# A fused attention and two-MoE kernel: the column transfers of the first chunk put ahead of the transfers of x

## The chip, the cores and the metric

The kernel runs on one core of one Trainium2 chip. The metric is the device time of an execution in microseconds (us). The core has five engines that each run their own instructions in program order: TensorE (PE; its weight loads are listed apart as PEld), VectorE (DVE), ScalarE (ACT), GpSimd (POOL) and SyncE (SP). Nearly all data transfers (DMAs) are issued by SP, in SP's order. Each of SP's transfers signals one of eight completion counters, taken in turn and named DMAHW0 to DMAHW7 in the order rows below; a transfer that takes a counter waits until the transfer that had it before has landed.

## The reference

Attention with 4 batches, 8 heads, 576 positions and 64 channels, where heads 0 to 3 see the last 32 positions and heads 4 to 7 every 32nd one; then a dense MoE layer with a squared ReLU; then a routed layer of 8 experts of which each token takes one:

```python
def _moe2_ref(x, w_gate, w_output_gate, w1, w2):
    logits = x @ w_gate
    e_idx = np.argmax(logits, axis=1)
    ...
    eom = 1.0 / (1.0 + np.exp(-(x @ w_output_gate)))
    out = np.zeros((N, D), dtype=np.float32)
    for e in range(E):
        mask = e_idx == e
        ...
        h = np.maximum(x[mask] @ w1[e], 0.0)
        ye = h @ w2[e]
        out[mask] = gate_w[mask, None] * eom[mask, e, None] * ye
    return out

x = attention(q, k, v) as (2304, 512)
h = x @ w_in
r = np.maximum(h, 0.0)
x = (s * (r * r) + b) @ w_out
out = _moe2_ref(x, ...)
```

## The kernel before

The 2304 tokens are cut into five units of 256, 512, 512, 512 and 512 (`USZ`). Attention and the dense layer run unit by unit; each unit's result x goes to DRAM as `xd[u]` (line 1528). Matmuls are in float32 split in two parts, three products for each.

The routed layer bets on one expert. After the third unit the kernel takes the expert that most tokens chose and runs *all* tokens through that expert's weights (`dense`, from line 1924). For units 1 to 4 the first of its two matrix products is done in seven products of half size (M1 to M7, `product`, line 1975), which DVE and ACT combine (`combine`, line 1858). Such a stage on TensorE is: M1 and M6 of a stage, two products with the second matrix for the stage before (line 1940), M7 and M5, one more of those, M2, M4 and M3, and one more. On DVE a stage is `su` (line 1883), `dd` (lines 1886, 1889 and 1894) and the `ht` of line 1847. M7 waits for `su` of line 1883, and the next stage's M1 for the buffer that `dd` of line 1894 frees. Four stages make a unit; those of unit 2, the third one, lie around the change.

The operands of a unit come from `load_x` (line 1777): two transfers `xr` from `xd[s]` (line 1804), four sums `tt` on DVE (line 1818), and splits of them (lines 1661 and 1665) that the seven products read.

Tokens of other experts are then done in chunks of 32 (`SLOT`). `index` (line 2089) builds on DVE and TensorE a table of 80 columns, one for each chunk: `gid` has the token numbers, `sid` the places to write to, both in DRAM (lines 2192 and 2193). `li` holds the expert of each chunk and the number of chunks; its first column goes to DRAM as `lsd` (line 2204) and comes back as the row `lrow` (line 2205), from which the loop at the end takes a chunk's expert. `extra` (line 2209) does a chunk: it loads all of x into `X1` with five transfers (line 2213), reads the chunk's expert, loads the chunk's column as `gr` (line 2219), four times as `gc` (line 2221) and once from `sid` (line 2222), makes addresses `gs` on DVE (lines 2227 to 2229) for a gather by POOL, copies the 32 tokens out of `X1` into `xe` in eight groups of four (line 2242), each after a read of four numbers of `gr`, loads the expert's weights `we` in eight transfers (line 2249) into the buffer that `X1` had, and multiplies (lines 2260 to 2290). The first chunk is part of the schedule (`first_extra`, line 2302); any others follow in a loop (line 2358), which on this input has no turn.

The order of the work is not written out. `body` runs its parts as generators: each `yield op(...)` names an engine, a duration and the events waited for, and `Order` (line 211) keeps a clock for each engine and lets the part go on whose next step can start first, corrected by a priority. The order so found, with durations that are the source's own, is the order in which each engine gets its instructions. An event is an `Ev` whose time is set by `o.set`.

Of the kernel before, what the change touches and what calls it, by code (L numbers as in the profile page):

```python
# [6 lines left out]
F32 = mybir.dt.float32  # L7
F32R = mybir.dt.float32r
I32 = mybir.dt.int32
# [5 lines left out]
DVE = mybir.EngineType.DVE  # L15
# [3 lines left out]
NT, DM, DFF, E, DFE = B * S, H * D, 2048, 8, 1024  # L19
NF2 = DFE // 128  # L20
QT = 128
USZ = (256, 512, 512, 512, 512)
UOF = tuple(sum(USZ[:k]) for k in range(len(USZ) + 1))
# [12 lines left out]
P = 128  # L36
# [5 lines left out]
KD = DM // P  # L42
NF = DFF // P
NU = len(USZ)
# [29 lines left out]
P_ATT2 = 0.1  # L74
P_GATE = -0.2
P_EXTRA = 0.3
P_EXTRA_PE = -0.3
GLAT = 0.5
P_SUMS = 0.2
# [117 lines left out]
DMA_LAT = 1.8  # L197
# [114 lines left out]
def op(*engs, waits=(), dep=True, on=(), late=0.0):  # L312
    return engs, waits, dep, on, late
# [6 lines left out]
def body(ctx, tc, qkv, w12, moe_s, moe_b, wg, e12, out):  # L320
    nc = tc.nc
# [6 lines left out]
    const = enter(tc.tile_pool(name="const", bufs=1))  # L328
    wp = enter(tc.tile_pool(name="w", bufs=2 * NF))
    mx = enter(tc.tile_pool(name="mx", bufs=2))  # L330
# [6 lines left out]
    xd = [dram.tile([P, KD, USZ[u]], F32, name=f"xd{u}") for u in range(NU)]  # L337
# [3 lines left out]
    lsd = dram.tile([P, 1], I32, name="lsd")  # L341
# [49 lines left out]
    o = Order()  # L391
# [71 lines left out]
    t_g, t_r, t_raw, t_x1, t_c = Tok(NG), Tok(NR), Tok(NRAW), Tok(1), Tok(1)  # L463
# [546 lines left out]
    ev_last = [Ev() for _ in range(NU)]  # L1010
# [644 lines left out]
    def parts(src, dst, late=0.0):  # L1655
        n = 1
        for x in src.shape[1:]:
            n *= x
        yield op(("ACT", n / 1200 + 0.2), ("DVE", n / 1400 + 0.06, P_DVE), late=late)
        if o.eng == "ACT":  # L1660
            nc.scalar.activation(out=dst[0], in_=src, func=AF.Copy)
        else:
            nc.vector.tensor_copy(out=dst[0], in_=src)
        yield op(("DVE", n / 960 + 0.15))
        nc.vector.tensor_sub(out=dst[1], in0=src, in1=dst[0].bitcast(F32))
# [103 lines left out]
    def x_tile(shape):  # L1769
        tok = [t for t in o.got if t in (t_xa, t_xb, *t_xc.values())][0]  # L1770
        for b in t_xc:
            if tok is t_xc[b]:
                return st[b], tok
        pool, n = (m2[0], NXA) if tok is t_xa else (m2b[0], NXB)
        return pool.tile(shape, F32R, name="x2", tag="x2", bufs=n), tok

    def load_x(s):
        n = USZ[s]
        hn = n // 2
        yield op(("SP", 0.0), waits=[ev_k[4 * NF + 8], ev_last[s]])  # L1780
        raws = []
        if s == 0:
            yield op(("DMA", 2 * n / 350), waits=[t_w])
            t = wp.tile([P, KD, n], F32, name="xr", tag="w")
            nc.sync.dma_start(out=t, in_=xd[s])
            ev = Ev()
            o.set(ev, o.fin + DMA_LAT + 1.0)
            for c, b in enumerate(t_xc):
                def go(c=c, b=b):
                    yield op(("SP", 0.0), waits=[ev, ev_kept], dep=False)  # L1790
                    x = st[b]
                    yield from parts(t[:, 2 * c:2 * c + 2, :], [x[:, h] for h in range(2)])
                    x2[s, c] = x
                    if len(x2) == 2:
                        o.free(t_w)
                        o.set(ev_x2[s, "X"])
                        o.spawn(load_x(1), prio=P_X2)

                o.spawn(go(), prio=P_X2)
            return  # L1800
        for c in range(2):
            yield op(("DMA", n / 350), waits=[t_w])
            t = wp.tile([P, 2, n], F32, name="xr", tag="w")
            nc.sync.dma_start(out=t, in_=xd[s][:, 2 * c:2 * c + 2, :])
            ev = Ev()
            o.set(ev, o.fin + DMA_LAT + 1.0)
            raws.append((t, ev))
        (r0, e0), (r1, e1) = raws
        src = {"B11": r0[:, :, 0:hn], "B21": r1[:, :, 0:hn], "B22": r1[:, :, hn:]}
        w = 2 * hn / 960 + 0.15  # L1810
        yield op(("DVE", w), waits=[e0, e1, t_g, t_g])
        tt = [mx.tile([P, 2, 2, hn], F32, name="tt", tag="g", bufs=NG) for _ in range(2)]
        for k, b in enumerate(("T1", "T2", "T3", "T4")):
            src[b] = tt[k // 2][:, k % 2]
        for k, (x, y) in enumerate(((r0[:, :, hn:], src["B11"]), (src["B22"], src["T1"]), (src["B22"], r0[:, :, hn:]), (src["B21"], src["T2"]))):
            if k:
                yield op(("DVE", w))
            nc.vector.tensor_sub(out=tt[k // 2][:, k % 2], in0=x, in1=y)
        for b in OPS:
            yield op(("SP", 0.0), waits=[[t_xa, t_xb, *t_xc.values()]])  # L1820
            x, x_tok[s, b] = x_tile([P, 2, 2, hn])
            x2[s, b] = x

            def go(b=b, x=x):
                yield op(("SP", 0.0))
                yield from parts(src[b], [x[:, h] for h in range(2)])
                o.set(ev_x2[s, b])
                src.pop(b)
                if not src:
                    for _ in range(2):  # L1830
                        o.free(t_w)
                        o.free(t_g)
                    if s + 1 < NS:
                        o.spawn(load_x(s + 1), prio=P_X2)

            o.spawn(go(), prio=P_X2)
# [247 lines left out]


    ex = {}
    ev_idx = Ev()

    def index():
        yield op(("POOL", 2.5))  # L2090
# [71 lines left out]
        for t in range(0, NQT + 2, 2):  # L2162
            if t < NQT:
                yield op(("DVE", 0.5), waits=[t_w])
                ow = wp.tile([P, 1024], F32R, name="ow", tag="w")
                for k in range(2):
                    a = ow[0:QT, k * 512:k * 512 + SLOT]
                    c = ow[0:QT, k * 512 + SLOT:k * 512 + SLOT + NTAB]
# [22 lines left out]
        yield op(("DMA", 1.0))  # L2191
        nc.sync.dma_start(out=gid, in_=gi)
        nc.sync.dma_start(out=sid, in_=si2)
        yield op(("DVE", 0.7))
        before = tb[0:QT, 888:888 + E - 1]
        nc.vector.tensor_scalar(out=before, in0=end[:, 0:E - 1], scalar1=jc, scalar2=None, op0=ALU.is_le)
# [2 lines left out]
        li = const.tile([P, 2], I32, name="li")  # L2199
        nc.vector.tensor_copy(out=li[:, 0:1], in_=ej)  # L2200
        nc.vector.tensor_copy(out=li[:, 1:2], in_=end[:, E - 1:])
        yield op(("DMA", 3.0))
        lrow = const.tile([1, P], I32, name="lrow")
        nc.sync.dma_start(out=lsd, in_=li[:, 0:1])
        nc.sync.dma_start(out=lrow, in_=lsd.rearrange("(o s) c -> o (s c)", o=1))
        ex["li"], ex["lrow"] = li, lrow
        o.spawn(first_extra(), prio=P_EXTRA, pe=P_EXTRA_PE)

    def extra(col, get, n=NT):
        src = mx.tile([P, KD, NT], F32, name="X1", tag="big", bufs=1)  # L2210
        for u in range(NU):
            yield op(("DMA", 1.7), waits=[ev_last[u]])
            nc.sync.dma_start(out=src[:, :, UOF[u]:UOF[u + 1]], in_=xd[u])
        yield op(("DMA", 3.0))
        e = get()
        gr = mx.tile([1, SLOT], I32, name="gr", tag="gr", bufs=1)
        gc = mx.tile([P, 2], I32, name="gc", tag="gc", bufs=1)
        with nc.allow_non_contiguous_dma(reason="one column of a table"):
            nc.sync.dma_start(out=gr, in_=col(gid).rearrange("s o -> o s"))
            for h in range(NROW):  # L2220
# [10 lines left out]
        se = mx.tile([P, 1], F32, name="se", tag="se", bufs=1)  # L2231
        nc.gpsimd.indirect_dma_start(out=se, out_offset=None, in_=scd,
                                     in_offset=bass.IndirectOffsetOnAxis(ap=gs[:, 2:3], axis=0))
        yield op(("DVE", 1.8), waits=[t_r])
        xe = mx.tile([P, KD, SLOT], F32, name="xe", tag="r", bufs=NR)
        for k in range(0, SLOT, 4):
            if k:
# [5 lines left out]
        big = mx.tile([P, NF2, 1024], F32, name="we", tag="big", bufs=1)  # L2243
        we = []
        evs = []
        for fc in range(NF2):
            yield op(("DMA", 1.46))
            t = big[:, fc, :]
            nc.sync.dma_start(out=t, in_=e12[bass.ds(e * NF2 + fc, 1)].rearrange("o p f -> p (o f)"))
            we.append(t)  # L2250
            evs.append(Ev())
            o.set(evs[-1], o.fin + DMA_LAT)
        hp = None
        for k in range(NF2 // NROW):
            yield op(("PE", 1.0), waits=[evs[NROW * k + NROW - 1]] + ([t_att] if k == 0 else []))
# [39 lines left out]
        if n < NT:  # L2295
# [3 lines left out]
                                     in_=oe, in_offset=None, bounds_check=n - 1, oob_is_err=False)  # L2299
        o.free(t_g)  # L2300

    def first_extra():
        li = ex["li"]
        yield from extra(lambda t: t[:, 0:1], lambda: sp_value(li[0:1, 0:1], E - 1), NT - P)
# [31 lines left out]
    with tc.manual_schedule():  # L2336
        prep()
        o.filler = filler
        o.pe_cold = PE_COLD
        o.spawn(load_qkv(0), after=False)  # L2340
        o.spawn(load_w64(0), after=False)
        o.spawn(attn(0), prio=P_ATT, after=False)
        o.spawn(masks(1), after=False)
        o.spawn(split_w64(0), prio=P_SPLIT, after=False)
        o.spawn(moe1(), after=False)
        o.spawn(split_x0(), after=False, prio=P_X0)
        o.spawn(open_st(), after=False)
        o.spawn(make_ops(STR[0]), prio=P_OPS, after=False)
        o.spawn(open_m2(), after=False)
        o.spawn(make_sums(0), after=False, prio=P_SUMS)  # L2350
        if WARM:
            o.spawn(warm(), after=False, prio=P_WARM)
        o.spawn(load_x(0), prio=0.1, after=False)
        o.run()
    n = nc.values_load(ex["li"][0:1, 1:2], min_val=0, max_val=NTAB, skip_runtime_bounds_check_because=why)
    o.got = [t_att[0]]
    att_bank()
    with tc.For_i(1, n, 1) as j:
        lrow = ex["lrow"]
# [90 lines left out]
```

## Time and profile before

| | |
|---|---|
| median of 3 runs | 676.94 us (676.92 to 678.75) |
| profiled execution | 675.04 us |
| its span, from the first to the last instruction | 673.3 us |
| PE busy | 660.1 us (98%) |
| PEld busy | 570.7 us (85%) |
| DVE busy | 423.8 us (63%) |
| ACT busy | 317.7 us (47%) |
| granted TensorE clock | 1.000 |
| DMA | 83.81 MB, mean 124 GB/s |

Busy time is a mean over the span; a stretch in which an engine waits has to be looked for in the views by time. Times in those views count from the span's start. In a row of the timeline the first two numbers are start and duration of a group of equal instructions, xN their number, and the brackets at the end give how long the engine sat idle before it and what ended that. SPq rows are the issues of transfers: their duration is that of the issue, not of the transfer.

### The profile page before, as it was taken

The page shows a single profiled execution, that of the slowest core. Times are in us where ns is not written, and L with a number is a line of the kernel's source. Part 1 is how long each engine was busy: PE and PEld are TensorE (multiplying, and loading weights), DVE is VectorE, ACT ScalarE, POOL GpSimd, SP SyncE. Part 2 cuts the span into 40 slices and gives each one's busy share as a digit, 9 for nine tenths or more (in the row PEclk, how much of TensorE's full clock was granted, in tenths as well). Part 3 has the DMA queues.
Part 4 walks back from the last instruction along what each step waited for, and adds up shares of the span by engine and source line. Part 5 has one row for each costly group of instructions (what it writes and reads, how often), then busy time and mean ns, then how long its engine had stood idle before and what let it go on. Part 6 is the DMA issues. An engine that isn't in the chain of part 4 may idle for free. (4 is left out here: it accounts for less than half of the span.)

```text
span 673.3 us, 14007 instructions
## 1 busy us (share of the span) xinstructions
PE 660.1 (98%) x5346; PEld 570.7 (85%) x5346; DVE 423.8 (63%) x998; ACT 317.7 (47%) x855; POOL 39.1 (6%) x135
## 2 busy tenths in 40 slices
PE   9999999999999999999999999999999989999996
PEld 7788888898777778788899888998888878988995
DVE  5998878744465575476585768777587446525540
ACT  5877566665674564353343545544332323314311
POOL 7750000000000000000000000000000000000000
PEclk9999999999999999999999999999999999999999
DMA  8984246332543453422311143223200290530201
GB/s 304 406 322 129 91 132 208 128 129 89 186 164 110 141 169 92 154 87 66 109 33 40 63 157 118 94 76 119 80 33 1 70 369 33 187 126 10 87 1 65
DMA packets 40823, 83.81 MB, mean 124 GB/s; under 512 B 6701, under 2 KB 20142, under 8 KB 39986
## 3 DMA queue, kind: packets, MB, share of 16 engines
q1 hardware_dynamic: 40658, 82.87, 36.4%
q8 instruction: 43, 0.70, 0.4%
q14 instruction: 26, 0.21, 0.1%
q0 software_dynamic: 96, 0.02, 0.0%
HBM read 64.11 MB, written 15.63 MB: 118 GB/s over the span
## 5 line engine op out<-in xcount | busy, mean ns | idle before, releaser
L1071 PE MATMUL h<-xsl,w 128*128 128x512 f32 (+1 forms) x492 | 110.8, 371 | 0.0
L1105 PE MATMUL bk<-g,w 128*128 128x512 f32 (+1 forms) x480 | 107.2, 370 | 0.0
L1166 PE MATMUL bk<-g,w 128*128 128x512 f32 x396 | 102.2, 393 | 0.0
L1071 PEld LDWEIGHTS h<-xsl,w 128*128 128x128 f32 x492 | 84.7, 188 | 15.8 <-issue 0.4
L1940 PE MATMUL bk<-w,ht 128*128 128x512 f32 x384 | 96.2, 392 | 0.0
L1105 PEld LDWEIGHTS bk<-g,w 128*128 128x128 f32 x480 | 82.5, 188 | 16.0 <-ACT g L1043 0.8
L1166 PEld LDWEIGHTS bk<-g,w 128*128 128x128 f32 x396 | 69.9, 188 | 11.6
L1940 PEld LDWEIGHTS bk<-w,ht 128*128 128x128 f32 x384 | 68.6, 188 | 11.9 <-issue 0.4
L1019 ACT ACTIVATE r<-h 128x512 f32<-128x512 f32 (+1 forms) x48 | 25.3, 527 | 73.1 <-PE h L1071 67.6
L1045 DVE TENSOR_TENSOR g<-r,g 128x512 fp32r<-128x512 f32 (+1 forms) x41 | 25.9, 633 | 37.7 <-ACT g L1043 37.7
L1418 PEld LDWEIGHTS h<-xsl,w 128*128 128x128 f32 x336 | 45.2, 190 | 4.9 <-issue 0.8
L1418 PE MATMUL h<-xsl,w 128*128 128x256 f32 x336 | 46.7, 282 | 0.0
L1845 ACT ACTIVATE ht<-h 128x256 fp32r<-128x256 f32 x24 | 9.2, 384 | 76.6 <-PE h L1982 51.9
L829 ACT ACTIVATE pr<-pr,sm 128x64 f32<-128x64 f32 (+2 forms) x102 | 32.8, 323 | 0.3
L1043 ACT ACTIVATE g<-r 128x512 fp32r<-128x512 f32 (+1 forms) x41 | 23.9, 584 | 1.7
L1886 DVE TENSOR_TENSOR dd<-h,su 128x256 f32<-128x256 f32 x16 | 6.8, 424 | 28.5 <-PE h L1982 28.5
L1982 PE MATMUL bk<-x,wc 128*128 128x256 f32 x168 | 24.4, 282 | 0.0
L1418 PE MATMUL h<-xsl,s 128*128 128x256 f32 x168 | 24.3, 279 | 0.0
L1418 PEld LDWEIGHTS h<-xsl,s 128*128 128x128 f32 x168 | 22.6, 188 | 1.1
L1031 ACT ACTIVATE r<-r 128x512 f32<-128x512 f32 (+1 forms) x39 | 22.9, 588 | 1.2
L1910 ACT ACTIVATE ob<-bk,scl 128x512 f32<-128x512 f32 x17 | 11.7, 688 | 22.6 <-PE bk L1940 22.0
L1982 PEld LDWEIGHTS bk<-x,wc 128*128 128x128 f32 x168 | 21.8, 189 | 0.0
(305 smaller groups left out, 1135.4 us busy)
## 6 DMA issues: line engine op xcount, KB each, us to landing
raw<-w SPq DMA_DIRECT2D x32, 512.0 KB, 7.5
qkv<-qkv SPq DMA_DIRECT2D x14, 512.0 KB, 4.5
xr<-xd SPq DMA_DIRECT2D x9, 512.0 KB, 4.5
qkv<-qkv SPq DMA_DIRECT2D x8, 544.0 KB, 4.5
out<-ob SPq DMA_DIRECT2D x17, 256.0 KB, 2.0
xd<-x SPq DMA_DIRECT2D x4, 1024.0 KB, 5.2
sraw<-sd SPq DMA_DIRECT2D x16, 256.0 KB, 2.7
wraw<-e SPq DMA_DIRECT2D x16, 256.0 KB, 2.9
```

The lines of the kernel that those rows point to most:

```text
L829: nc.scalar.activation(out=ps4[:, h, i, :], in_=ps4[:, h, i, :], func=AF.Exp, scale=0.125, bias=v[2][:, j:j + 1], accum_out=v[1][:, j:j + 1])
L1019: nc.scalar.activation(out=r, in_=h, func=AF.Relu)
L1031: nc.scalar.activation(out=to, in_=r, func=AF.Square)
L1043: nc.scalar.activation(out=gt[:, 0, 0:U], in_=r, func=AF.Copy)
L1045: nc.vector.tensor_sub(out=gt[:, 1, 0:U], in0=r, in1=gt[:, 0, 0:U].bitcast(F32))
L1071: nc.tensor.matmul(out=h, lhsT=w_t[2 * fc][:, a, c * P:(c + 1) * P], rhs=xt(u, c, x), start=(c == 0 and n == 0), stop=(c == KD - 1 and n = ...
L1105: nc.tensor.matmul(out=acc[pu][c], lhsT=w_t[2 * pf + 1][:, a, c * P:(c + 1) * P], rhs=gt[:, x, 0:cols(pu)], start=(first and n == 0), stop ...
L1166: nc.tensor.matmul(out=acc[pu][c], lhsT=w_t[2 * pf + 1][:, a, c * P:(c + 1) * P], rhs=pbox[0][:, x, 0:cols(pu)], start=(begin and i == 0), ...
L1418: nc.tensor.matmul(out=out_, lhsT=weights(x, a, c), rhs=o_place(u, b)[y][:, c], start=(first and c == 0 and n == 0), stop=(name in ("M2", ...
L1910: nc.scalar.activation(out=ob, in_=src, func=AF.Copy, scale=scl[:, i:i + 1])
L1940: nc.tensor.matmul(out=acc2[s, t][0], lhsT=box[k][:, x, t * P:(t + 1) * P], rhs=w_t["p", 2 * f + 1][:, a, :], start=(f == 0 and n == 0), s ...
L1982: nc.tensor.matmul(out=banks[to], lhsT=t[:, a, off + c * P:off + (c + 1) * P], rhs=x2[s, b][:, y, c, :], start=(first and c == 0 and n == ...
```

## The change

In `extra` the read of the expert and the transfers of `gr` and `gc` come first, now after an event `ev_gid` for the table in DRAM; the five transfers of x follow behind the gather and wait for an event `ev_raw`, which `load_x` sets for unit 2, the third one (`EARLY_X`), when its `xr` are issued. In the planner's clock a transfer of x now lasts by its size, and the copies `xe` wait for an event of x. `lrow` is no longer loaded in `index` but in `extra`, behind the weights of the first chunk.

```diff
+EARLY_X = 2
...
         (r0, e0), (r1, e1) = raws
+        if s == EARLY_X:
+            o.set(ev_raw, e1.t - 1.0)
...
-    ev_idx = Ev()
+    ev_gid, ev_raw = Ev(), Ev()
...
         nc.sync.dma_start(out=sid, in_=si2)
+        o.set(ev_gid, o.fin + DMA_LAT + 0.4)
...
-        yield op(("DMA", 3.0))
-        lrow = const.tile([1, P], I32, name="lrow")
+        ex["li"] = li
+        yield op(("DMA", 0.5))
         nc.sync.dma_start(out=lsd, in_=li[:, 0:1])
-        nc.sync.dma_start(out=lrow, in_=lsd.rearrange("(o s) c -> o (s c)", o=1))
-        ex["li"], ex["lrow"] = li, lrow
         o.spawn(first_extra(), prio=P_EXTRA, pe=P_EXTRA_PE)
 
     def extra(col, get, n=NT):
-        src = mx.tile([P, KD, NT], F32, name="X1", tag="big", bufs=1)
-        for u in range(NU):
-            yield op(("DMA", 1.7), waits=[ev_last[u]])
-            nc.sync.dma_start(out=src[:, :, UOF[u]:UOF[u + 1]], in_=xd[u])
-        yield op(("DMA", 3.0))
+        yield op(("DMA", 4.2), waits=[ev_gid])
         e = get()
...
-        yield op(("DVE", 1.8), waits=[t_r])
+        src = mx.tile([P, KD, NT], F32, name="X1", tag="big", bufs=1)
+        for u in range(NU):
+            yield op(("DMA", USZ[u] / 180), waits=[ev_last[u], ev_raw])
+            nc.sync.dma_start(out=src[:, :, UOF[u]:UOF[u + 1]], in_=xd[u])
+        ev = Ev()
+        o.set(ev, o.fin + DMA_LAT + 1.0)
+        yield op(("DVE", 1.8), waits=[t_r, ev])
...
+        if n < NT:
+            yield op(("DMA", 0.5))
+            ex["lrow"] = const.tile([1, P], I32, name="lrow")
+            nc.sync.dma_start(out=ex["lrow"], in_=lsd.rearrange("(o s) c -> o (s c)", o=1))
```

What this does to the order of the engines shows in three places. Lines have other numbers there: `tt` 1821, `su` 1886, `dd` 1889, 1892 and 1897, `ht` 1850, `gs` 2225 to 2227. The first place is SP's queue from `lsd` on, with the counters and engines that each row waits for; before:

```order
L2204 DMA lsd<-li 128x1 [waits DMAHW2_49,DVE_49]
L2205 DMA lrow<-lsd 1x128 [waits DMAHW3_49,DMAHW2_49]
L1804 DMA xr<-xd_78 128x1024 [waits DMAHW4_49,PE_49,Activation_49]
L1804 DMA xr<-xd_78 128x1024 [waits DMAHW5_49,PE_49]
L1915 DMA out<-ob 128x512 [waits DMAHW6_49,Activation_49]
L2213 DMA X_6375<-xd_75 128x4x256 [waits DMAHW1_49,DMAHW0_49,DMAHW7_49,DVE_49,Pool_49]
L1915 DMA out<-ob 128x512 [waits Activation_49]
L2213 DMA X_6375<-xd_76 128x4x512
```

and with the change:

```order
L2208 DMA lsd<-li 128x1 [waits DMAHW2_49,DVE_49]
L1654 TENSOR_LOAD li [waits DVE_49]
L2217 DMA gr<-gid 1x32x1 [waits DMAHW3_49,DMAHW0_49]
L2219 DMA gc<-gid 32x1 [waits DMAHW4_49]
L2219 DMA gc<-gid 32x1 [waits DMAHW5_49]
L2219 DMA gc<-gid 32x1 [waits DMAHW6_49]
L2219 DMA gc<-gid 32x1 [waits DMAHW7_49]
L2220 DMA gc<-sid 32x1 [waits DMAHW1_49]
L1805 DMA xr<-xd_78 128x1024 [waits PE_49,Activation_49]
L1805 DMA xr<-xd_78 128x1024 [waits DMAHW2_49,PE_49]
L1918 DMA out<-ob 128x512 [waits DMAHW3_49,Activation_49]
L1918 DMA out<-ob 128x512 [waits DMAHW4_49,Activation_49]
```

`lrow`, which waited for the landing of `lsd` (DMAHW2), is gone from here; `gr` and `gc` stand ahead of `xr`, X has moved behind a second store, and the second `xr` now takes the counter of `lsd`.

The second place is DVE in the stage in which these transfers are issued; before:

```order
L1886 TENSOR_TENSOR dd<-h,su 128x256
L1889 TENSOR_TENSOR dd<-bk_3576,dd 128x256
L1818 TENSOR_TENSOR tt<-xr 128x512
L1818 TENSOR_TENSOR tt<-xr,tt 128x512
L1894 TENSOR_TENSOR dd<-h,su 128x256
L1847 SCALAR_TENSOR_TENSOR ht<-h,ht 128x256
L1877 TENSOR_TENSOR su<-bk_3576,su 128x256
L1818 TENSOR_TENSOR tt<-xr 128x512
```

and with the change:

```order
L1892 TENSOR_TENSOR dd<-bk_3576,dd 128x256
L2225 TENSOR_SCALAR gs<-gc 128x1
L2226 TENSOR_SCALAR gs<-gc 128x1
L2227 SCALAR_TENSOR_TENSOR gs<-gs 128x1
L1897 TENSOR_TENSOR dd<-h,su 128x256
L1850 SCALAR_TENSOR_TENSOR ht<-h,ht 128x256
L1880 TENSOR_TENSOR su<-bk_3576,su 128x256
L1821 TENSOR_TENSOR tt<-xr 128x512
L1850 SCALAR_TENSOR_TENSOR ht<-dd,ht 128x512
L1850 SCALAR_TENSOR_TENSOR ht<-su,ht 128x256
L1821 TENSOR_TENSOR tt<-xr,tt 128x512
L1821 TENSOR_TENSOR tt<-xr 128x512
```

Between the second and the third `dd` stand now the three `gs` in place of two `tt`, which follow behind the first `ht`.

The third place is DVE one stage on; before:

```order
L1847 SCALAR_TENSOR_TENSOR ht<-su,ht 128x256
L2227 TENSOR_SCALAR gs<-gc 128x1
L2228 TENSOR_SCALAR gs<-gc 128x1
L2229 SCALAR_TENSOR_TENSOR gs<-gs 128x1
L1883 TENSOR_TENSOR su<-h,su 128x256
L2239 TENSOR_LOAD gr
L2242 ISA
L2242 COPY xe<-X_6375 128x4
```

and with the change:

```order
L1850 SCALAR_TENSOR_TENSOR ht<-su,ht 128x256
L1886 TENSOR_TENSOR su<-h,su 128x256
L1889 TENSOR_TENSOR dd<-h,su 128x256
L1892 TENSOR_TENSOR dd<-bk_3576,dd 128x256
L2243 TENSOR_LOAD gr
L2246 ISA
L2246 COPY xe<-X_6464 128x4
```

The `gs` are gone from here, and the first group of copies has moved behind two `dd`. Of the eight groups, which stood at 1, 2, 2, 1, 1 and 1 in the gaps that follow each other, there are now 1, 2, 1, 1, 2 and 1, from one gap later on, the last one behind two more `dd` than before. On TensorE the 32 products of `we` and `xe` (line 2260, now 2268), which had M6 of a stage between their halves, stand behind it in one piece; on ACT one `ob` has changed places with an `ht`.

## Rows read from the trace of the kernel before

**Rows 1.** Waits of TensorE by who ended them: total us, times, longest.

```profile
PE h L1982 <- DVE dd L1894: 2.6, 1, 2.6
PE h L1982 <- DVE su L1883: 1.8, 2, 1.4
```

**Rows 2.** Timeline around TensorE's first stall: TensorE and DVE, 533 to 546 us.

```profile
533.42 0.42 DVE L1889 TENSOR_TENSOR dd<-bk,dd 128x256 f32<-128x256 f32 x1 [0.28 <-PE bk L1982]
...
536.70 1.52 PE L1940 MATMUL bk<-w,ht 128*128 128x512 f32 x6
...
537.30 0.69 DVE L1818 TENSOR_TENSOR tt<-xr 128x512 f32<-128x512 f32 x1 [3.46 <-DMA xr<-xd]
...
539.70 0.69 DVE L1818 TENSOR_TENSOR tt<-xr,tt 128x512 f32<-128x512 f32 x1 [1.70 <-DMA xr<-xd]
540.31 0.42 DVE L1894 TENSOR_TENSOR dd<-h,su 128x256 f32<-128x256 f32 x1
...
540.78 0.97 PE L1982 MATMUL h<-xb,wa 128*128 128x256 f32 x6 [2.56 <-DVE dd L1894]
...
545.00 0.87 PE L1982 MATMUL h<-x,wc 128*128 128x256 f32 x6
```

**Rows 3.** Timeline of SP's issues, 525 to 549 us.

```profile
525.21 0.34 SPq L2204 DMA_DIRECT2D lsd<-li  x1
532.39 0.27 SPq L2205 DMA_DIRECT2D lrow<-lsd  x1
532.78 1.13 SPq L1804 DMA_DIRECT2D xr<-xd  x2
...
542.83 1.20 SPq L2213 DMA_DIRECT2D X<-xd  x2
...
545.76 2.97 SPq L2221 DMA_DIRECT2D gc<-gid  x4
```

**Rows 4.** Transfers from 475 us on: number, KB each, median us from issue to landing.

```profile
X<-xd SPq DMA_DIRECT2D x4, 1024.0 KB, 9.1
...
xr<-xd SPq DMA_DIRECT2D x6, 512.0 KB, 4.4
...
gid<-ix SPq DMA_DIRECT2D x1, 10.0 KB, 1.4
...
lsd<-li SPq DMA_DIRECT2D x1, 0.5 KB, 7.2
...
gr<-gid SPq DMA_DIRECT2D x1, 0.1 KB, 10.3
```

**Rows 5.** Timeline around TensorE's second stall, 556 to 557 us.

```profile
556.11 0.15 DVE L2227 TENSOR_SCALAR gs<-gc 128x1 int32<-128x1 int32 x1 [4.53 <-DMA gc<-gid]
...
556.44 0.42 DVE L1883 TENSOR_TENSOR su<-h,su 128x256 f32<-128x256 f32 x1
...
556.92 0.97 PE L1982 MATMUL h<-x,wc 128*128 128x256 f32 x6 [1.37 <-DVE su L1883]
```

**Rows 6.** Timeline: the start of line 1886 on DVE in five stages.

```profile
532.71 0.42 DVE L1886 TENSOR_TENSOR dd<-h,su 128x256 f32<-128x256 f32 x1 [2.93 <-PE h L1982]
...
545.91 0.42 DVE L1886 TENSOR_TENSOR dd<-h,su 128x256 f32<-128x256 f32 x1 [1.45 <-PE h L1982]
...
557.93 0.43 DVE L1886 TENSOR_TENSOR dd<-h,su 128x256 f32<-128x256 f32 x1
...
568.30 0.42 DVE L1886 TENSOR_TENSOR dd<-h,su 128x256 f32<-128x256 f32 x1 [1.55 <-PE h L1982]
...
578.69 0.42 DVE L1886 TENSOR_TENSOR dd<-h,su 128x256 f32<-128x256 f32 x1 [2.30 <-PE h L1982]
```

**Rows 7.** Timeline: last group of copies, last five weight issues, first use's second half.

```profile
575.87 0.52 DVE L2242 COPY xe<-X 128x4 f32 x4
...
585.56 2.58 SPq L2249 DMA_DIRECT2D we<-e  x5
...
597.12 1.08 PE L2260 MATMUL bk<-we,xe 128*32 128x128 f32 x32
```

## The prediction

> **What bounds the kernel.** I read the page first: TensorE is busy for nearly the whole span, so a microsecond counts only where TensorE waits. The view of TensorE's waits names few, and the two longest lie in the stretch that the change touches [rows 1]: 2.6 us for DVE's `dd` of line 1894 and, among two waits for `su` of line 1883, one of 1.4. The timeline shows what kept DVE. At 533.84 (533.42 + 0.42) it is done with line 1889, and the next two instructions in its order are the `tt` of line 1818, which need the operands `xr` of the fourth unit; these land at 537.30 and 539.70, so the `dd` behind them runs at 540.31 and TensorE goes on at 540.78 [rows 2]. Why `xr` is late stands in SP's queue: `lsd` is issued at 525.21, its landing takes 7.2 us, and `lrow`, which reads it back, holds the queue until 532.39; only then is `xr` issued [rows 3, 4]. The second stall is one stage on: the three `gs` stand ahead of `su`, wait for the small column `gc` until 556.11, and TensorE goes on at 556.92 [rows 5]. `gc` is late since it is issued at 545.76, behind the five transfers of X [rows 3], and lands behind them.
>
> What both cost is read from the pace of TensorE's stages, by the starts of line 1886 [rows 6]: 13.20 and 12.02 us for the two disturbed stages, 10.37 and 10.39 for the next two. The excess is 2.81 + 1.63 = 4.44 us. The waits alone, 2.56 [rows 2] and 1.37 [rows 5], make 3.93; I take 4.44, because the stages do the same products and the pace also holds the slow first products behind a stall.
>
> **The change, part by part.**
>
> *`lrow` leaves the place behind `lsd`.* SP's hold from 525.55 (525.21 + 0.34) to 532.39 ends [rows 3]. No engine reads `lrow` before the loop behind the schedule, so its new place behind the weights costs nothing: one issue of 0.27 [rows 3] on a queue that then only waits for ACT's next `ob`.
>
> *The small transfers come up.* Ahead of `xr` now stand the read of `li`, `gr`, four `gc` and the `gc` from `sid`. Between the end of the X issues (542.83 + 1.20 = 544.03) and the first `gc` (545.76) the read of `li` and `gr` took 1.73, the four `gc` 2.97 [rows 3], partly waiting; with 0.4 for the last that is 5.1 at most. So the columns are issued from 525.55 to 530.7 or sooner, and the first `xr` by then instead of at 532.78. The second `xr` reuses the completion counter of `lsd` (DMAHW2 in the order), so it still waits for 532.4; that is at least one issue, some 0.8 us, earlier than before. Those behind it in SP (stores, X) keep about their time.
>
> *`gs` takes the place of the two `tt` on DVE.* It is reached at 533.84. TensorE's products of the stage run until 538.2 (536.70 + 1.52) [rows 2]; `dd` needs 0.42 [rows 2] and the three `gs` 0.33 (556.11 to 556.44) [rows 5], so a `gc` that lands by 537.4 costs nothing. How long the columns take with nothing large ahead no row shows. From below there is `gid`, a table of 32 pieces, with 1.4; from above `gr` with 10.3, which had X ahead of it; `lsd`, of small pieces too, took 7.2 [rows 4]. For the last `gc`, issued by 530.3, these give 531.7, 540.6 and 537.5. I take the low end: the column has 32 pieces as `gid` has, and the 10.3 were queueing. Gain: the whole 2.81.
>
> *The `tt` move behind `dd`.* The first one is reached at about 537.7. `xr` with its 4.4 [rows 4] lands at 535.1, and no later than the 537.30 of before. The second is reached at about 538.9; its `xr`, by 532.4 + 4.4, lands at 536.8, at the latest at the 539.70 of before. Behind it stand one more `tt` and `su`, 0.69 + 0.68 + 0.42, and `su` is wanted 4.2 us after the first product of the new stage (540.78 to 545.00) [rows 2], so at 542.2 with that product at 538.0. Even 539.70 leaves 0.7 us. So `xr` is what is late next, and it costs nothing.
>
> *`gs` leaves the second place.* `su` follows `ht` at once. The loss of 1.63 goes; nothing else on DVE waits for a transfer there.
>
> *The copies `xe` move back.* The first group now stands behind line 1892 of the third stage and waits for all of X. X is issued as before or sooner, since the stores between its parts wait for ACT, whose `ob` come earlier without the stall. With the last issue at about 541 and 9.1 us [rows 4] X has landed by 550; the group is reached at 557.93 - 4.44 + 0.85 = 554.3. Slack 4 us.
>
> *The loop's own new order* does nothing here: no instruction of it is in the trace, as one chunk holds all tokens.
>
> Sum: 4.44 us less, between 1.3 (`gc` at 540.6: it holds TensorE until some 541.4 where 538.2 was due, so 3.2 come back) and 4.44. The profiled execution, 675.04 us with a span of 673.3, becomes 670.6. Its time lies 1.90 under the median of the runs, 676.94, so for the median I say 672.5.
>
> **Rivals.**
>
> *A. The columns sit behind `lsd`.* On SP's rings `lsd` is ahead of them, and it is not done until 532.4. If they land only after it and then take as long as it did, `gc` is there at 532.4 + 7.2 = 539.6, `dd` ends at 540.35 instead of 540.73 [rows 2], and the first stall stays but for 0.4. Gain 0.4 + 1.63 = 2.0: 674.9 us. For it: `gr` did land behind X, so a queue is kept. Against it: pieces of 4 bytes that only read the table need not take what a write to DRAM took. The Trainium skill's page "DMA: Bandwidth & Descriptors", section "Queues, rings and completion order", speaks against this change: an engine's increment of a semaphore lands only after every earlier write of that DMA engine, so by it no `gc` is told of before `lsd`'s 532.4. By that rule alone 532.4 is still ahead of the 533.84 at which DVE asks, and the sum stays 4.44; no row of the trace before has a small read right behind `lsd`. Chance 0.12.
>
> *B. The weights of the chunk become late.* They share the buffer with X. The last group of copies ran from 575.87 to 576.39 [rows 7], ahead of the `dd` at 578.69 [rows 6]; now one more group stands there and the last one behind two `dd`, so it ends at about 580.0 by the old clock (578.69, two `dd` of 0.42, a group of 0.52). Against TensorE the first weights slip by up to 3.6 us. The last five are issued from 585.56 behind a store that moves with TensorE, and TensorE asks at 597.12 without a wait [rows 7], so a slip of the first ones is mostly hidden. If two thirds of it came through, 2.4 us, the gain is 2.0: 674.9 us. Chance 0.06.
>
> *C. The small transfers go one after another.* `gs` now stands in DVE's order ahead of a `dd` that TensorE needs, so each microsecond that `gc` lands after 537.4 is one of TensorE's, and from 537.4 + 4.44 = 541.9 on the kernel is slower than before. If each of the six took the 7.2 of `lsd`, in turn behind it, `gc` would land at 532.4 + 43.2 = 575.6, and the kernel lose 575.6 - 541.9 = 33.7: 710.6 us. Against it: `gr` landed at 555.3 (10.3 after an issue at 545.0) and `gs`, which needs all four `gc`, began at 556.11 [rows 4, 5]; four came in under a microsecond. Chance 0.04, most of it for smaller delays than that.
>
> That the change doesn't open the queue at all is true of the second `xr` alone, and priced above at nothing.
>
> **The numbers.** The forecast, that both stalls go, has 0.78; A 0.12, B 0.06, C 0.04. Its time is 672.5. The range goes from 671.0, which leaves 1.5 for the scatter that the profiled execution shows below the median, to 675.2, which takes in A and B; outside lie C, the rest of the upper bound (675.6) and a little below. A measurement of this kernel tells 0.3% from no change, about 2.0 us: the forecast's 4.4 is 0.66%, while A and B lie on that edge. Faster: 0.78 and 0.06 of A and B, 0.84; same 0.12; slower 0.04.
>
> **What would show it.** In the profile after: `gr` and `gc` issued between 526 and 531, and no transfer `lrow` there; the three `gs` before 535; line 1897 near 536.5; TensorE without a wait over 0.5 us between 530 and 560; starts of line 1889 10.4 apart throughout; the `tt` without a wait that passes on to `su`; the first `xe` copies near 554, not waiting for X. The prediction is wrong if `gs` is seen to wait past 537.4 (A or C), if the merged 32 products of `we` and `xe` are preceded by a wait of TensorE (B), or if the pace of 10.4 comes back and the time does not follow it.

## The result, and the profile after

| | before | with the change |
|---|---|---|
| median | 676.93 us (6 runs) | 671.69 us (6 runs, 670.20 to 672.09) |
| ratio | | 0.9919, 95% interval 0.9900 to 0.9937 |
| profiled execution, its span | 675.04, 673.3 us | 671.69, 669.9 us |
| starts of the stages' first `dd`, three stages from the disturbed one on | 13.20, 12.02, 10.37 apart [rows 6] | 10.39, 10.38, 10.39 apart |

The changed kernel is faster by 5.2 us in the medians (0.63 to 1.00% of the time). Forecast were 4.4 us and 672.5 us.

TensorE's waits after the change, by who ended them (total us, times, longest); the two that led [rows 1] are gone:

```profile
PE bk L693 <- DVE pr L673: 1.5, 1, 1.5
...
PE h L1985 <- DVE su L1886: 0.4, 1, 0.4
PE bk L2268 <- DMA we<-e: 0.3, 1, 0.3
```

The first lies in the attention at the start; the second was there before too (the smaller of two for `su`); the third, TensorE waiting for the chunk's weights, is new.

SP's issues and the landings (number, KB each, median us from issue) show the new order, against [rows 3, 4]:

```profile
525.10 0.34 SPq L2208 DMA_DIRECT2D lsd<-li  x1
525.90 0.55 SPq L2217 DMA_DIRECT2D gr<-gid  x1
526.50 2.19 SPq L2219 DMA_DIRECT2D gc<-gid  x4
528.75 2.27 SPq L2220 DMA_DIRECT2D gc<-sid  x1
531.12 1.32 SPq L1805 DMA_DIRECT2D xr<-xd  x2
```

```profile
X<-xd SPq DMA_DIRECT2D x4, 1024.0 KB, 8.2
...
xr<-xd SPq DMA_DIRECT2D x6, 512.0 KB, 5.0
...
gc<-gid SPq DMA_DIRECT2D x4, 0.1 KB, 4.7
...
gr<-gid SPq DMA_DIRECT2D x1, 0.1 KB, 6.3
```

SP no longer stands from 525.55 to 532.39. The columns are out by 531, the first `xr` follows at 531.12, the second once `lsd`'s counter is free. `gr` takes 6.3 us from issue to landing and the last `gc` 4.7, not 1.4. By the counters' records `lsd` lands at 532.04, `gr` at 532.21 and the four `gc` between 532.38 and 532.95, each 0.17 to 0.2 us behind the one ahead.

The timeline of DVE and TensorE where the two stalls were, against [rows 2, 5, 6]:

```profile
532.60 0.42 DVE L1889 TENSOR_TENSOR dd<-h,su 128x256 f32<-128x256 f32 x1 [2.93 <-PE h L1985]
...
533.65 0.14 DVE L2225 TENSOR_SCALAR gs<-gc 128x1 int32<-128x1 int32 x1
...
536.08 0.42 DVE L1897 TENSOR_TENSOR dd<-h,su 128x256 f32<-128x256 f32 x1 [2.03 <-PE h L1985]
...
537.13 0.68 DVE L1821 TENSOR_TENSOR tt<-xr 128x512 f32<-128x512 f32 x1
...
537.95 0.87 PE L1985 MATMUL h<-xb,wa 128*128 128x256 f32 x6
...
542.08 0.87 PE L1985 MATMUL h<-x,wc 128*128 128x256 f32 x6
...
542.99 0.42 DVE L1889 TENSOR_TENSOR dd<-h,su 128x256 f32<-128x256 f32 x1 [2.10 <-PE h L1985]
...
553.37 0.42 DVE L1889 TENSOR_TENSOR dd<-h,su 128x256 f32<-128x256 f32 x1 [2.93 <-PE h L1985]
```

`gs` runs at 533.65 with no bracket, so `gc` was there. The `dd` at 536.08 waits for TensorE's product and no longer TensorE for it; the product at 537.95 has no idle time ahead. Both stages take the undisturbed 10.39.

Between the two profiles the pace in this stretch gives 4.43 us (the starts from 532.71 to 568.30 before, 532.60 to 563.76 after), the forecast's 4.44. Yet the medians are 5.2 apart, and the spans of these two executions 3.4: of the missing microsecond 0.40 is lost at the chunk's weights (run 4 below), and the time behind DVE's last operation is 0.8 us longer after than before. So two questions were left: where the median's larger gain comes from, and what each half of the change does.

### The profile page after: what moved, and what is told of

Read it like the earlier page. It is cut to its first block, busy times and chain, and to the rows that moved or that the text cites. A ratio compares the mean times of both kernels' runs of the same rounds, so it can differ in the third digit from the quotient of the medians.

```text
span 669.9 us, 14009 instructions
## 1 busy us (share of the span) xinstructions
PE 658.0 (98%) x5346; PEld 569.3 (85%) x5346; DVE 424.8 (63%) x998; ACT 318.0 (47%) x855; POOL 40.0 (6%) x135
## 5 line engine op out<-in xcount | busy, mean ns | idle before, releaser
L1333 ACT ACTIVATE g<-rr 128x256 fp32r<-128x256 f32 x32 | 13.3, 417 | 18.1 <-DVE rr L1326 18.0
L1333 ACT ACTIVATE g<-dd 128x512 fp32r<-128x512 f32 x16 | 10.1, 631 | 24.9 <-DVE dd L1326 24.9
```

What stands on the lines that cost most here:

```text
L1333: nc.scalar.activation(out=dst[:, 0, :], in_=tmp, func=AF.Copy)
```

## The experiments

All ratios are against the kernel before, run on the same chip. The traces do not hold every record of the completion counters; a landing "by the counters" is the last record that is there. Run 1 to run 6 are the experiments by their numbers.

**1. `lrow` alone.** The kernel before, `lrow` taken from behind `lsd`:

```diff
         nc.sync.dma_start(out=lsd, in_=li[:, 0:1])
-        nc.sync.dma_start(out=lrow, in_=lsd.rearrange("(o s) c -> o (s c)", o=1))
...
+        if n < NT:
+            ex["lrow"] = const.tile([1, P], I32, name="lrow")
+            nc.sync.dma_start(out=ex["lrow"], in_=lsd.rearrange("(o s) c -> o (s c)", o=1))
```

> The kernel before, with lrow alone taken from behind lsd and put behind the weights; the columns stay behind X. My theory: the two stalls have two causes, lrow's hold of SP (2.81 us) and the columns' place behind X (1.63). xr is issued at about 525.6 instead of 532.78, the tt of line 1818 do not wait, and TensorE has no wait for dd of line 1894. The gs stay ahead of su and wait for gc: it landed at 556.1, and comes 2.8 to 4.7 us earlier (the stores that X waits for move by 2.8, and the 1 MB of xr is out of the way), while the moment it is wanted moves by 2.8, so a wait of TensorE for su of 0 to 1.4 us is left. Time 672.5 to 674.1, ratio 0.9934 to 0.9958. Rival 1, one cause for both: with SP free the columns come in time too, no wait for su, ratio as the change's 0.992. Rival 2, the columns' place is all that matters: 676.9, ratio 1.000.

Measured: 674.74 us, ratio 0.9968 (0.9953 to 0.9982). SP, DVE and TensorE in the timeline:

```profile
526.48 1.52 SPq L1804 DMA_DIRECT2D xr<-xd  x2
...
534.57 0.69 DVE L1818 TENSOR_TENSOR tt<-xr 128x512 f32<-128x512 f32 x1
538.21 0.69 DVE L1818 TENSOR_TENSOR tt<-xr,tt 128x512 f32<-128x512 f32 x1 [2.94 <-DMA xr<-xd]
...
539.29 0.96 PE L1982 MATMUL h<-xb,wa 128*128 128x256 f32 x6 [0.27 <-DVE dd L1894]
...
554.82 0.15 DVE L2225 TENSOR_SCALAR gs<-gc 128x1 int32<-128x1 int32 x1 [4.73 <-DMA gc<-gid]
...
555.63 0.97 PE L1982 MATMUL h<-x,wc 128*128 128x256 f32 x6 [1.58 <-DVE su L1883]
```

The two causes are separate, as the theory had it: the first stall shrinks to a stage of 10.90 us, the second stays (12.23, 1.84 over 10.39). It gained less than expected for a reason that the theory had left out: `xr`, now issued right behind `lsd`, is held by it. `lsd` lands at 534.02 by the counters, the two `xr` at 534.54 and 538.11, 8 and 11 us after their issue, so the second `tt` still waits. With 1 MB of `xr` queued, little moves meanwhile (us, busy TensorE, granted clock, DMA share, GB/s):

```profile
529.00:531.00 2.00, 2.00 (x14) 1.00 1.48 68
531.00:533.00 2.00, 2.00 (x12) 1.00 0.62 23
```

**2. The columns alone.** The changed kernel, `lrow` back behind `lsd`:

```diff
         nc.sync.dma_start(out=lsd, in_=li[:, 0:1])
+        lrow = const.tile([1, P], I32, name="lrow")
+        nc.sync.dma_start(out=lrow, in_=lsd.rearrange("(o s) c -> o (s c)", o=1))
...
-            nc.sync.dma_start(out=ex["lrow"], in_=lsd.rearrange("(o s) c -> o (s c)", o=1))
```

> The changed kernel with lrow back directly behind lsd; the columns stay ahead of xr and X. My theory: SP is held until 532.4 again, the columns are issued from 532.7 to about 538 and the last gc from gid lands at 538 to 540, past the 537.4 at which it begins to cost; xr follows at 538.2 and lands at about 542.6 and 543.5, past what su needs. So a stall of 2.5 to 3.5 us stands where the first one was, and the second one is gone: 675 to 676.2, ratio 0.997 to 0.999. Rival, the columns' place alone makes the gain: ratio 0.992.

Measured: 675.51 us, ratio 0.9978 (0.9966 to 0.9989), inside the first theory's numbers. Timeline, and the landings of the columns:

```profile
538.17 0.15 DVE L2228 TENSOR_SCALAR gs<-gc 128x1 int32<-128x1 int32 x1 [3.79 <-DMA gc<-gid]
...
538.96 0.96 PE L1985 MATMUL h<-xb,wa 128*128 128x256 f32 x6 [0.21 <-DVE dd L1897]
...
542.38 0.69 DVE L1821 TENSOR_TENSOR tt<-xr 128x512 f32<-128x512 f32 x1 [2.81 <-DMA xr<-xd]
...
543.72 2.11 PE L1943 MATMUL bk<-w,ht 128*128 128x512 f32 x8 [2.19 <-DVE ht L1850]
```

```profile
gc<-gid SPq DMA_DIRECT2D x4, 0.1 KB, 1.6
...
gr<-gid SPq DMA_DIRECT2D x1, 0.1 KB, 1.9
```

The late `gc` costs 0.21 us; the larger wait is one that was not named: a `tt` stands ahead of two `ht`, waits for the late `xr`, and TensorE's product with the second matrix waits for the `ht`. The stage takes 13.36 us. With `lsd` already landed when they are issued, the columns take 1.6 and 1.9 us.

**3. `lsd` moved behind X.**

```diff
-        nc.sync.dma_start(out=lsd, in_=li[:, 0:1])
...
             nc.sync.dma_start(out=src[:, :, UOF[u]:UOF[u + 1]], in_=xd[u])
+        if n < NT:
+            nc.sync.dma_start(out=lsd, in_=ex["li"][:, 0:1])
```

> The changed kernel with the write lsd moved from ahead of the columns to behind the five transfers of X. My theory: what made the columns land 4.7 and 6.3 us after their issue was lsd, which landed only at 532.04; without it ahead gr and gc land within 2.5 us of their issue, at 529 or before, and the second xr is issued at once. Since gs is wanted only from 537.1 on, none of it reaches TensorE: time as the changed kernel's within 0.3% (ratio 0.990 to 0.994). Rival A in its other form, small reads are slow by themselves: 4.7 and 6.3 us stay though lsd is gone. Rival, earlier columns give more: ratio under 0.990.

Measured: 671.97 us, ratio 0.9919 (0.9906 to 0.9933). `gc` lands 1.7 us after its issue instead of 4.7, so it was `lsd` that held the columns, and the time does not gain by their coming earlier. But it has a cost of its own one place on:

```profile
558.59 0.52 DVE L2247 COPY xe<-X 128x4 f32 x4 [3.78 <-DMA X<-xd]
```

The copies wait for X, and that stage takes 11.19 us. Windows of the same kernel (us, busy TensorE, granted clock, DMA share, GB/s):

```profile
552.00:554.00 2.00, 2.00 (x16) 1.00 1.64 174
554.00:556.00 2.00, 2.00 (x14) 1.00 0.21 18
```

The last packets of X are through at 553.0, its counter is full only at 558.4, and at 554 to 556 hardly a byte moves although `xr` is queued. In the changed kernel X had landed at 553.65. `lsd` stands right behind X here, so it holds up the report of a transfer ahead of it too; how it does that, the records do not tell.

**4. The kernels themselves again**, for their profiles. Unchanged.

> The changed kernel once more, as the measure beside the three others on the same chip. My theory: the pace of the stages gives 4.4 us, the weights take back 0.4, so the ratio is 0.9935 to 0.9945 (672.6 to 673.2). Against it the first measurement, 0.9919: if it comes out so again, about 1 us of the gain is outside the stretch with the two stalls.

> The kernel before once more, for a second profile of it: its first one, 675.04 us, lies some 2 us under the median of its 29 times, so the pace of two stalled stages read from it, 13.19 and 12.02 against 10.39, may not be the usual one. If the stalls are of one size each time and the scatter sits elsewhere (the first loads of qkv at the start), the two stages come out within 0.2 of that and the sum of the rest is longer. If the usual stalls are larger (the gain measured, 5.2 to 6.0 us, against the 4.1 of the two profiles), their excess over 10.39 is 5.5 to 6.5 instead of 4.44.

> The kernel before a third time, for the same question: two profiles tell a usual size from a single one.

> The changed kernel a third time, on the same chip as the two above. By the profiles of before the usual stalled stage costs 4.96 to 5.17 us (not 4.44), and the 64 products in one piece save 0.32 or lose 0.39 at the weights: a gain of 4.6 to 5.5, ratio 0.9919 to 0.9932.

Measured: the changed kernel 671.14 us, ratio 0.9911 (0.9895 to 0.9927), and 671.60, ratio 0.9931 (0.9910 to 0.9952). The kernel before 676.54 and 677.04 in the two profiled executions. Part of the median's larger gain is here. TensorE and DVE in the first of them:

```profile
532.72 0.42 DVE L1886 TENSOR_TENSOR dd<-h,su 128x256 f32<-128x256 f32 x1 [2.93 <-PE h L1982]
...
541.57 1.65 PE L1982 MATMUL h<-xb,wa 128*128 128x256 f32 x6 [3.35 <-DVE dd L1894]
543.02 1.48 PE L1982 MATMUL h<-x,wc 128*128 128x256 f32 x6
544.30 3.23 PE L1940 MATMUL bk<-w,ht 128*128 128x512 f32 x12
547.37 0.87 PE L1982 MATMUL h<-x,wc 128*128 128x256 f32 x6
...
548.28 0.42 DVE L1886 TENSOR_TENSOR dd<-h,su 128x256 f32<-128x256 f32 x1 [2.64 <-PE h L1982]
...
556.22 0.15 DVE L2227 TENSOR_SCALAR gs<-gc 128x1 int32<-128x1 int32 x1 [2.27 <-DMA gc<-gid]
...
558.66 0.42 DVE L1886 TENSOR_TENSOR dd<-h,su 128x256 f32<-128x256 f32 x1 [0.62 <-PE h L1982]
```

and its windows:

```profile
540.00:542.00 2.00, 0.43 (x2) 0.88 1.07 393
542.00:544.00 2.00, 2.00 (x11) 0.50 1.05 408
544.00:546.00 2.00, 2.00 (x10) 0.77 1.06 405
546.00:548.00 2.00, 2.00 (x13) 1.00 1.04 391
```

TensorE's first stall is 3.35 us here where it was 2.56 [rows 2], and behind it the granted clock is 0.50, that is 1.2 GHz for 2.4: six products last 1.65 and 1.48 instead of 0.87. From the first of them to the product of 547.37 go 5.80 us, 4.13 in the changed kernel (537.95 to 542.08). So this one stage takes 15.56 us, 5.17 over 10.39: 3.35 of waiting, and nearly all of the rest in products at the lower clock. `gc` comes at the same moment as before, 556.22 against 556.11 [rows 5], but everything is 2.4 us later now: `gs` still waits, TensorE does not, and the next stage takes 10.38. The other execution gives 15.35 and 10.38, and this stall:

```profile
542.21 1.65 PE L1982 MATMUL h<-xb,wa 128*128 128x256 f32 x6 [3.17 <-DVE dd L1894]
```

Its span and this one's are 1.5 to 1.9 us longer than the first profile's.

Both later executions, then, pay 4.96 to 5.17 us in one stage, not 2.81 and 1.63 in two; in the first profile `xr` came 0.7 us earlier (537.30 against 537.97) and the clock stayed at 1.00. That these two are the usual ones rests on more than their number: 675.04 us, the time of the first profile, lies below all 53 other times of this kernel (675.29 to 679.79). Of the 45 unprofiled ones with a granted clock on record 40 have 0.996 or less, where the first profile has 1.000 and these two 0.995. Where in those 40 the clock was lower is not recorded; a wait at the start can lower it too (last section).

The changed kernel's two new profiles have all these stages at 10.39 and differ from the first in the weights:

```profile
591.38 1.29 PE L2268 MATMUL bk<-we,xe 128*32 128x128 f32 x38
593.01 1.06 PE L2268 MATMUL bk<-we,xe 128*32 128x128 f32 x26 [0.33 <-DMA we<-e]
```

is the first profile, with a stage of 13.22 us; this is the second:

```profile
592.05 1.96 PE L2268 MATMUL bk<-we,xe 128*32 128x128 f32 x64
```

with 12.50, as in the third. Before, with M6 between the two halves, it was 12.82 in all three. The 64 products in one piece save 0.32 us, or lose 0.40 when the last weight is late.

**5. More writes ahead of the columns.** The changed kernel with one, or three, more tables like `lsd` written behind it, which nobody reads:

```diff
+    lsx = [dram.tile([P, 1], I32, name=f"lsx{k}") for k in range(3)]
...
         nc.sync.dma_start(out=lsd, in_=li[:, 0:1])
+        for t in lsx:
+            nc.sync.dma_start(out=t, in_=li[:, 0:1])
```

> The changed kernel with one more write like lsd (128 pieces of 4 bytes to a DRAM table of its own, which nobody reads) right behind lsd, ahead of the columns. My theory: a transfer on SP's rings lands only behind those ahead of it, and TensorE pays from the moment gc lands past 537.1 (dd must end by 537.95). If two such writes take their 7 us one after the other, gc lands at 537 to 540 and the second xr, whose counter is that of the new write, is issued at 536 to 539 and lands at 540.5 to 543.5: a stall of 0.5 to 3 us, 672.5 to 675. Rival, the two writes overlap: both land at about 533, no stall, ratio as the changed kernel's, 0.991 to 0.992.

> The same with three more writes. One after the other: gc at 545.5 (4.2 for each more) to 554 (7 for each), the second xr landing at 545 to 550, a stall of 8 to 17 us in the stage of the first one: 679 to 688, slower than before. Overlapping: gc at 533 to 535, time within 1.5 us of the changed kernel's. In either case each us that gc lands past 537.1 should be one of TensorE's; this is rival C's mechanism made on purpose.

Measured with one: 671.83 us, ratio 0.9922 (0.9895 to 0.9950): the rival held. The two writes land together, at 532.22 and 532.54 by the counters. `gc` landed at 535.39, `gs` ran at once, and the stage took 10.39:

```profile
535.42 0.16 DVE L2228 TENSOR_SCALAR gs<-gc 128x1 int32<-128x1 int32 x1 [1.94 <-DMA gc<-gid]
```

Measured with three: 680.48 us, ratio 1.0040 (1.0023 to 1.0057), slower than before.

```profile
541.97 0.15 DVE L2228 TENSOR_SCALAR gs<-gc 128x1 int32<-128x1 int32 x1 [8.66 <-DMA gc<-gid]
...
542.77 1.65 PE L1986 MATMUL h<-xb,wa 128*128 128x256 f32 x6 [5.08 <-DVE dd L1898]
...
547.91 3.78 PE L1944 MATMUL bk<-w,ht 128*128 128x512 f32 x8 [0.51 <-DVE ht L1851]
```

Neither expectation held as put, though the time lies in the first one's range: the first two writes land together, at 532.02 and 532.71 by the counters, the third and fourth, whose counters the two `xr` wait for, only at about 540 and 541. So `gc` comes 4.8 us past the 537.1 of the expectation. The stage takes 20.48 us, 10.09 too many: 5.08 and 0.51 of waits, and nearly as much again in products at the lower clock (six in 1.65; eight in 3.78 where twelve took 2.88). "Each us that `gc` is late is one of TensorE's" was too little: here it was two.

**6. The weights in one piece.** The changed kernel with all eight weights issued together, two stores behind them:

```diff
-            yield op(("DMA", 1.46))
+            if fc == 0:
+                yield op(("DMA", 1.46 * NF2))
...
-            o.set(evs[-1], o.fin + DMA_LAT)
+            o.set(evs[-1], o.fin + DMA_LAT + 2.0)
```

and, in a second kernel, `lsd` moved behind the last two `xr` as well:

```diff
-        nc.sync.dma_start(out=lsd, in_=li[:, 0:1])
...
+        if s == EARLY_X + 2:
+            nc.sync.dma_start(out=lsd, in_=ex["li"][:, 0:1])
```

> The changed kernel with its eight weight transfers issued in one piece, the two stores that stood between them behind them. Rival B in small: in the changed kernel the last weight lands within 1 us of TensorE's 64 products of we and xe, and in one profile of two they waited (stage of 13.21 us, in the other 12.50; before 12.82 in each profile). My theory: issued from 576.2 on without a store between, all eight are out by 581 and land by 590, the stage takes 12.50 and no product of we waits: 0.0 to 0.7 less than the changed kernel, not to be told in the time (671 to 672). Against it: the two stores come some 4 us later, ACT's ob lack their buffers and TensorE waits for a bank, 0.5 to 1.5 us more.

> The same, and the write lsd moved behind the last two transfers of xr, where SP has nothing to issue for 20 us. My theory: the columns land 2 us after their issue, nothing waits behind lsd (behind X it held up X's landing, and the copies waited until 558.59), the stages are 10.39 and the stage of the weights 12.50: the changed kernel's best profile each time, 670.5 to 671.5. Rival: as the slack at gs is there already, no difference from the changed kernel; either is within the scatter, so the rows decide.

Measured: 670.58 us, ratio 0.9918 (0.9898 to 0.9937), and 671.90, ratio 0.9923 (0.9901 to 0.9946); neither can be told from the changed kernel. In the first the last weight lands at 589.5, the products begin at 591.13, and the stage takes 12.50: the stores' delay cost nothing. The last weight has 1.6 us to spare here, where in the first profile of the changed kernel the products waited for it; that the wait never comes, one profile does not show. The second missed its expectation: `lsd` stands three transfers behind X and holds it all the same.

```profile
559.25 0.52 DVE L2247 COPY xe<-X 128x4 f32 x4 [4.67 <-DMA X<-xd]
```

By the counters 15 of the 16 rings have reported X by 552.7, the last one at 559.08. That stage takes 12.09 us, 1.70 lost. For `lsd`, the place that the change left it in is the best of the three by the stages; the times do not tell them apart.

## Why the prediction was right, and where not

The sign, the place and the mechanism were right, and 671.69 lies in the range; a size was off.

- *SP's hold and the second `xr`.* Right: columns from 525.90, first `xr` at 531.12, the second only after `lsd`'s counter at 532.04 (forecast: 532.4).
- *`gs` ahead of `dd`.* The result was right, the reason not. I took the columns' price from `gid`'s 1.4; they took 4.7 and 6.3. They need only 1.6 to 1.9 by themselves (runs 2 and 3), and for the rest they stood behind `lsd`, which is rival A's premise. But A let them take another 7.2 behind it, and they landed within 0.9 us of it. The page "DMA: Bandwidth & Descriptors" of the Trainium skill, section "Queues, rings and completion order", has the counter's increment wait for earlier writes of that DMA engine; the records agree, with 0.17 to 0.2 us between landings. What saved the step was not the price but the slack: 532.95 against 537.1, of which run 5 used up 2.4 us at no cost.
- *`tt` and X.* The `tt` cost nothing, as said. X was thought to have 4 us of slack; its last part landed at 553.65 instead of 550, and DVE was free for the first copies at 554.50, so 0.85 us were left. The 0.56 us of idle time ahead of the copies at 555.06 are no wait for X: the kernel before has 0.48 there as well (run 4's profile, 557.46).
- *Rival B* is true in small: its sign, a wait at the merged products, is there with 0.33 us, and 0.40 us were lost in one profile of three, 0.32 won in two. Its 2.4 us did not come. (The products are 64, two halves of 32, not 32 as said there.)
- *Rival C* did not occur, and run 5 shows that its mechanism is real, at about twice the price given.
- *The term that was mis-sized is the sum's 2.81 + 1.63 = 4.44, as carried over to the median.* I saw that the profiled execution lay 1.90 under the median and subtracted the same 4.44 from both. The runs show that this 1.90 was in part the stalls themselves, 0.63 us of it: the two later executions pay 5.07 (mean of 5.17 and 4.96) in one stage. Most of the 1.90 lies elsewhere. The two stalls were not two items to add. A longer first one costs the clock as well and hides the second; `gc` comes 23.3 to 23.5 us after the stage's first `dd` in all three profiles of the kernel before. With 5.07, and 0.32 won or 0.40 lost at the weights, the gain is 4.7 to 5.4, against 4.7 to 6.0 by the three ratios. (The lower end of the sum's range is 4.44 - 3.2 = 1.24, not 1.3; nothing hangs on it.)

Of the halves, `lrow`'s move alone gave 2.2 us and the columns' move alone 1.5, together less than the whole, since each leaves a wait standing: 0.51 + 1.84 are left over in the one, 2.97 in the other, and 5.07 less these is 2.7 and 2.1 (1.7 with the 0.36 that the second loses at the weights).

What stays open: why the first profile's `lsd` landed 0.4 to 0.5 us sooner after its issue (7.16 us against 7.64 and 7.58), and why the clock fell in the two profiles with the longer stall and not in the first: that the length of the stall decides it is not shown (last section). The rest of the scatter lies outside the stretch: at the start, where TensorE's waits for `qkv` add up to between 0.5 and 3.6 us in these profiles, and behind DVE's last operation, where the end of two executions differs by up to 0.8 us.

## What to carry to other kernels

Look at more than one profile before adding up stalls: a wait that ends at a moment of its own (here `gc`, at 556.1 and 556.2 in two profiles whose stages were 2.4 us apart) is hidden when an earlier one grows, and the sum of one execution is not the sum of another. A stall of TensorE can cost its length and then a slower clock on top, so the durations of the products behind it belong to its price. Take a blocking read-back out of a shared queue first, then ask what the write ahead of it still holds: its transfers may be small and its hold on the queue long.

## What the runs showed of the hardware that was not expected

A write of 512 bytes to DRAM in 128 pieces of 4 bytes had its packets through in 0.2 us (525.94 to 526.13) and landed over the 16 rings from 527.88 to 532.04. While it does, the rings move little else: 68 and 23 GB/s at 529 to 533 us in run 1, 18 GB/s at 554 to 556 in run 3, each time with `xr` queued. Two such writes in a row land together (532.22 and 532.54); of four, two land at 532.02 and 532.71 and two at about 540 and 541.

The clock: after TensorE stood idle for 3.35, 3.17 and 5.08 us the granted clock fell (0.50 to 0.55 in the next window of 2 us); after 2.56 [rows 2] and 2.19 (run 2) it stayed at 1.00. The length of the idle time does not decide it alone, as the start of run 1's execution shows, where the clock fell after 2.46:

```profile
14.47 0.73 PE L636 MATMUL bk<-qkv 64*64 64x96 f32 x24 [2.46 <-DMA qkv<-qkv]
```

```profile
16.00:18.00 2.00, 2.00 (x24) 0.50 1.02 406
```

In the changed kernel's second profile it fell to 0.50 at 18 to 20 us, after 1.79 of idle time. What else decides, these runs do not show. The Trainium skill's page "TensorE: Matmul & The Clock Gate", section "HAM oscillation — how this bites in real kernels", says that a wait for a transfer can make the next burst start at the lower clock; the windows of run 4 agree.
